# A windowed attention and two expert layers on one core: the opening's instructions in a listed order, and a planner with re-measured costs

## The chip, the cores and the metric

The kernel runs on one core of one Trainium2 chip. The metric is the device time of one launch in microseconds (us). Five engines work beside each other, each taking its own instructions strictly in the order in which the program lists them: TensorE (PE in the profile; PEld is its weight load), VectorE (DVE), ScalarE (ACT), GpSimd (POOL) and SyncE (SP, which here only issues DMAs). An instruction that waits for another engine holds up everything listed behind it on its own engine.

## The reference

```
# attention: q, k, v are (2, 8, 768, 64); block = 32, window = 16
k_sum = max of k over blocks of 32 keys;  v_sum = mean of v over the same blocks
scores_l = q k^T / 8, kept only where |i - j| < 16
scores_s = q k_sum^T / 8 + log(32)
a = softmax over both together;  x = a [v ; v_sum]          # 1536 tokens x 512
# first layer
h = x @ w_in (512 x 2048);  x = (h * tanh(softplus(h))) @ w_out (2048 x 512)
# second layer
out = ((x @ w_a) * (x @ w_b)) @ w_out2                       # inner width 1536
```

The weights arrive as 64-bit floats and are brought to 32 bits on the chip, since nothing is computed on the host.

## The kernel before, in words

The 1536 tokens are cut into six groups g0 to g5 of 256 tokens, three for each of the two batch entries; the eight heads form four pairs p0 to p3. One unit of attention is a group and a head pair. A unit goes through all engines in turn:

- its keys and queries come by DMA (`load_k`, `load_q`), and VectorE takes the maximum over key blocks (L462, `prep_k`, one for each head pair of a batch entry);
- TensorE makes the scores (`batch_s`, L567 for the window, L571 for the block maxima): one call for each pair in g0, one for two pairs in the later groups;
- VectorE adds the mask and takes the row minimum, four times (L588); ScalarE makes four exponentials with row sums (L594); VectorE adds an epsilon (L597), inverts (L599) and multiplies (L601);
- TensorE transposes the weights (L626), ScalarE or VectorE copies them out of PSUM (L377 and L378, the two alternatives of `copy`), and TensorE multiplies them with v (L638, in g0 also L651 for the block means, which come from L492 through `keep_v`);
- ScalarE and VectorE split the result into a high and a low part (L377, L668), because every later product is made as three products of rounded parts.

The first layer runs on the finished groups: L897 is x times a chunk of w_in, L927 the activation Mish on ScalarE, L930 its split on VectorE, L944 the product with w_out. Its first four chunks are multiplied directly and interleave with the attention of later groups; the other chunks and the whole second layer use a scheme with seven products for eight (L1076, L1121, L1229). Each weight chunk is loaded raw, converted to 32 bits (L688 or L691 on ScalarE, L693 and L696 on VectorE) and split (L377 on ScalarE, L708 on VectorE).

ScalarE evaluates Mish and the exponential from different tables, and changing between them is an instruction of its own (ACT_TABLE_LOAD). At the start the program asks for the exponential's table once (`preload_act_table_set`, L426), so that the load lies before the first scores.

No order is written by hand. Every operation is handed to a class `Plan` (`add`) with a due time (`key`), its cost, what it reads and writes and the engines that may do it. `emit` then plays the program through with those costs: each engine takes, among the operations that are ready at its moment, the one with the smallest key, and that sets the instruction order for good. Where TensorE would be idle before a fixed moment (`fill_end`, 12.48 us of the planner's time), `emit` puts in dummy products (L434, `fill`) that keep it active; eight of them (`warm_up`) open the program. These dummies stand in the program unconditionally: the chip executes them whether TensorE would have waited or not. The constants at the head of `Plan` are the planner's picture of the chip: hops between engines, DMA delay and rate, table load, the clock of TensorE (`WARM`, `ham_end`).

## Time and profile before

| | us |
|---|---|
| median of 3 runs | 595.59 (595.39 to 595.86) |
| profiled execution, first to last instruction (span) | 593.8 |
| rest of a launch around the span (595.6 less 593.8) | 1.8 |
| PE busy in the span | 586.6 |
| DVE busy | 489.2 |
| ACT busy | 318.8 |

The profile does not give a measured time of its own for the profiled execution beside its span; the 1.8 us are the difference to the median of the runs. "Busy" for PE counts the dummies and also matmuls that run at a lower clock or wait inside the array, so a busy PE is not a PE that gets on.

### The profile page before, as it was taken

To read this page: it belongs to the slowest core of one execution; us is meant where nothing else is said; L and a number is where in the kernel's file an instruction comes from. 1 tells how busy PE (TensorE), PEld (TensorE's weight loads), DVE (VectorE), ACT (ScalarE), POOL (GpSimd) and SP (SyncE) were. 2 spreads that over 40 slices of the span, in tenths; PEclk is the share of its full clock that TensorE was granted. 3 is DMA by queue.
4 is the path that set the end of the run, shared out by engine and by line. 5 is a ranking of instruction groups with operands and counts; after the bars stand their busy time and mean duration, and the time that the engine had idled before them with its cause. 6 is when DMAs were issued, how large, how long until landed. Compare 5 with 4: busy or idle time off the path is not lost.

```text
span 593.8 us, 10770 instructions
## 1 busy us (share of the span) xinstructions
PE 586.6 (99%) x4162; PEld 530.9 (89%) x4163; DVE 489.2 (82%) x1134; ACT 318.8 (54%) x711; POOL 6.7 (1%) x34
## 2 busy tenths in 40 slices
PE   9999999999999999999999999999999999999998
PEld 5788788889898899989999999999898999999896
DVE  6899999999999988979799998858686876855443
ACT  5699999457555555455376655444262434433030
POOL 3000000000000000000000000000000000000000
PEclk9899999999999999999999999999999999999999
DMA  9997700222233221222003133230122212300202
GB/s 282 348 345 221 224 20 3 71 72 72 71 107 106 73 71 72 72 71 72 0 1 100 43 107 111 103 107 20 52 72 71 108 35 72 107 0 2 89 18 107
DMA packets 22288, 54.89 MB, mean 92 GB/s; under 512 B 1917, under 2 KB 8061, under 8 KB 22237
## 3 DMA queue, kind: packets, MB, share of 16 engines
q1 hardware_dynamic: 22236, 54.21, 27.8%
q8 instruction: 32, 0.52, 0.4%
q14 instruction: 20, 0.16, 0.1%
HBM read 50.07 MB, written 3.15 MB: 90 GB/s over the span
## 4 chain that ended last, share of the span: by engine, by line
PE 92%; ACT 3%; DVE 3%; DMA 1%; issue 1%; ACTq 0%
PE bank L1076 44%; PE bank L1121 17%; PE bank L1229 17%; PE bank L944 5%; PE bank L897 4%; ACT attn L594 2%; PE bank L567 1%; PE bank L638 1%; DMA attn<-attn 1%; PE bank L626 1%; PE bank L434 1%; DVE attn L588 1%; ACT L927 1%; ACT rounded L377 0%; PE bank L571 0%
## 5 line engine op out<-in xcount | busy, mean ns | idle before, releaser
L1076 PE MATMUL bank<-rounded,wext 128*128 128x384 f32 x1176 | 213.8, 335 | 0.0
L1076 PEld LDWEIGHTS bank<-rounded,wext 128*128 128x128 f32 x1176 | 205.7, 188 | 3.5
L377 ACT CAST rounded<-arena 128x384 fp32r<-128x384 f32 (+2 forms) x145 | 80.8, 568 | 88.9 <-PE bank L1229 37.4
L1121 PE MATMUL bank<-rounded,wext 128*128 128x512 f32 (+1 forms) x456 | 104.7, 380 | 0.0
L1229 PE MATMUL bank<-wext,rounded 128*128 128x512 f32 (+2 forms) x441 | 100.0, 386 | 0.0
L1089 DVE TENSOR_TENSOR arena<-arena,bank 128x384 f32<-128x384 f32 x132 | 71.8, 550 | 31.2 <-PE bank L1076 23.1
L1229 PEld LDWEIGHTS bank<-wext,rounded 128*128 128x128 f32 x441 | 82.0, 188 | 16.3
L1121 PEld LDWEIGHTS bank<-rounded,wext 128*128 128x128 f32 x456 | 83.9, 188 | 12.6
L1085 ACT COPY arena<-bank 128x384 f32<-128x384 f32 x108 | 51.5, 478 | 56.5 <-PE bank L1076 53.8
L377 ACT CAST wext<-arena 128x512 fp32r<-128x512 f32 (+1 forms) x80 | 49.0, 621 | 33.2 <-PE bank L1076 12.7
L1076 PE MATMUL bank<-rounded 128*128 128x384 f32 x336 | 61.1, 335 | 0.0
L1076 PEld LDWEIGHTS bank<-rounded 128*128 128x128 f32 x336 | 58.5, 188 | 0.2
L1125 DVE TENSOR_TENSOR arena<-bank,arena 128x512 f32<-128x512 f32 (+1 forms) x76 | 49.9, 658 | 10.0 <-PE bank L1121 9.9
L1248 DVE TENSOR_TENSOR arena<-bank,arena 128x512 f32<-128x512 f32 (+2 forms) x37 | 25.0, 677 | 34.5 <-PE bank L1229 34.5
L708 DVE TENSOR_TENSOR wext<-arena,wext 128x512 fp32r<-128x512 f32 (+1 forms) x80 | 49.8, 639 | 0.7 <-ACT wext L377 0.3
L696 DVE SCALAR_TENSOR_TENSOR arena<-arena 128x512 uint32<-128x512 uint32 x68 | 46.6, 689 | 2.3 <-ACT arena L688 0.4
L708 DVE TENSOR_TENSOR rounded<-arena,rounded 128x384 fp32r<-128x384 f32 (+2 forms) x72 | 40.9, 583 | 4.8 <-ACT rounded L377 4.3
L594 ACT ACTIVATE attn<-attn 128x120 f32<-128x120 f32 x96 | 36.7, 386 | 7.6 <-DVE attn L588 7.5
L944 PE MATMUL bank<-rounded 128*128 128x512 f32 (+1 forms) x168 | 37.1, 367 | 0.0
L688 ACT ACTIVATE arena<-arena 128x512 f32<-128x512 f32 x38 | 25.8, 680 | 17.7 <-DMA arena<-in_w_out_dram 9.4
L897 PE MATMUL bank<-rounded 128*128 128x512 f32 (+1 forms) x168 | 35.3, 363 | 0.0
L897 PEld LDWEIGHTS bank<-rounded 128*128 128x128 f32 x168 | 28.1, 189 | 4.7
(75 smaller groups left out, 546.3 us busy)
## 6 DMA issues: line engine op xcount, KB each, us to landing
arena<-in_w_out_dram SPq DMA_DIRECT2D x28, 512.0 KB, 3.3
arena<-in_w_in_dram SPq DMA_DIRECT2D x16, 512.0 KB, 3.9
arena<-in_w_a_dram SPq DMA_DIRECT2D x12, 512.0 KB, 4.1
arena<-in_w_b_dram SPq DMA_DIRECT2D x12, 512.0 KB, 3.3
arena<-in_kT_dram SPq DMA_DIRECT2D x8, 384.0 KB, 9.6
out_dram<-arena SPq DMA_DIRECT2D x11, 256.0 KB, 2.0
attn<-in_qT_dram SPq DMA_DIRECT2D x5, 512.0 KB, 8.7
attn<-in_v_dram SPq DMA_DIRECT2D x3, 768.0 KB, 7.3
```

The costliest lines, as they stand in the source:

```text
L377: alts = [("ACT", act_us(n), lambda env: nc.scalar.copy(out=dst(env), in_=src(env))), ("DVE", dve2_us(n) if fast else dve_us(n), lambda en ...
L594: act(key, SW + 90, lambda env, x=x: nc.scalar.activation(out=s[:, x, :], in_=s[:, x, :], func=AF.Exp, scale=-1.0, bias=negm[:, x:x + 1], ...
L696: dve(key, 512, lambda env: nc.vector.scalar_tensor_tensor(out=f.bitcast(U32), in0=hw.bitcast(U32), scalar=3, in1=f.bitcast(U32), op0=ALU. ...
L708: dve(key, n, lambda env: nc.vector.tensor_sub(out=r32(lo[0]()), in0=src, in1=hi[0]()), r=rd + hi[1], w=lo[1])
L897: nc.tensor.matmul(like(dst, b), lt, rt, start=(j == 0), stop=(j == 3 * KC - 1))
L944: nc.tensor.matmul(yp, lt, r32(rt), start=(fst and j == 0), stop=(lst and j == 2))
L1076: nc.tensor.matmul(dst, lt, r32(rt), start=(start and i == 0 and j == 0), stop=(last and i == 1 and j == 2), skip_group_check=True)
L1085: act(k, TN, lambda env: nc.scalar.copy(out=dst[0], in_=bank[env[nm[z]]][:, 0:TN]), w=[nm[z]] + dst[1])
L1089: dve(k, TN, lambda env: op(out=dst[0], in0=dst[0], in1=bank[env[nm[z]]][:, 0:TN]), w=dst[1] + [nm[z]], free=[nm[z]] if free else [])
L1121: nc.tensor.matmul(dst, lt, rt, start=(q == 0), stop=(q == 5))
L1125: dve(k + 1.2, n, lambda env: nc.vector.tensor_add(acc, bank[env[yn]][:, 0:n].rearrange(*shape[2], **shape[3]), acc), w=[yn] + ak, free=[yn])
L1229: nc.tensor.matmul(dst, lt, rt, start=(opens and j == 0), stop=(closes and j == n_mm - 1))
```

## The change

Two things change. First, `Plan` gets a table `ORDER` with a list of operation numbers for each engine. While an engine's list lasts, `emit` no longer chooses among the ready operations: the engine takes the next number of its list and waits for it if it is not ready. Operations in no list are not offered to any engine that still has a list to work off. The lists hold 125 operations for PE, 315 for DVE, 186 for ACT, 7 for POOL and 55 for SP; they cover the attention and the beginning of the first layer. After them the old rule goes on. In the lists an operation that ScalarE or VectorE may do is fixed to one of the two. SyncE's backlog limit is off while its list lasts, and dummies are put in on PE only while the next listed operation is waiting.

Second, the planner's constants and some durations are set to other values. They change no instruction by themselves, only what the planner believes, and so the placing of the dummies and the order after the lists. The explicit preload of the exponential's table, for instance, is now believed to cost 0.02 us instead of 1.3.

```
-    HOP = {"PE": 0.25, "DVE": 0.14, "ACT": 0.14, "POOL": 0.1, "SP": 0.05}
+    HOP = {"PE": 0.05, "DVE": 0.13, "ACT": 0.13, "POOL": 0.1, "SP": 0.05}
+    BEGIN = {"DVE": 0.93, "PE": 0.5, "ACT": 0.8}
-    DMA_LEAD, DMA_TAIL, DMA_RAMP = 0.62, 2.18, 8.0
+    DMA_LEAD, DMA_TAIL, DMA_RAMP = 0.62, 1.87, 8.3
-    TABLE, TABLE_PENALTY = 1.3, 5.37
-    WARM, PAGE, PE_LEAD, FETCH, FETCH_BUSY = 0.34, 256, 64, (6.4, 2.6), 46.0
+    TABLE, TABLE_PENALTY = 1.283, 5.37
+    WARM, PAGE, PE_LEAD, FETCH, FETCH_BUSY = 0.45, 256, 64, (6.4, 2.6), 46.0
...
-        ham_cold, ham_busy, ham_over, ham_end = True, 0.0, 0.0, 3.4133
+        ham_cold, ham_busy, ham_over, ham_end = True, 0.0, 0.0, 2.034
+        given = {e: list(reversed(q)) for e, q in dict(self.order).items()}
+        listed = {i: e for e, q in given.items() for i in q}
...
+                if given.get(e):
+                    i = given[e][-1]
+                    wq, rq = ([], []) if missing[i] else ([], [(0.0, i)]) if ready_at[i] <= t else ([(ready_at[i], 0.0, i)], [])
...
-                    until = dma_free - self.BACKLOG
+                    until = 0.0 if given.get(e) else dma_free - self.BACKLOG
...
+ORDER = {
...
+    "ACT": [
+        44, 45, 43, 42, 54, 57, 56, 55, 3, 87, 68, 69, 66, 81, 67, 80, 79, 78, 466, 105, 469, 33,
...
-    pl = Plan()
+    pl = Plan(ORDER)
...
-    pl.add(-1.0, [("ACT", 1.3, lambda env: nc.scalar.preload_act_table_set("exp_and_others"))], table="exp")
+    pl.add(-1.0, [("ACT", 0.02, lambda env: nc.scalar.preload_act_table_set("exp_and_others"))], table="exp")
```

Lines of the changed kernel stand 57 further down from the table on (L594 is L651 there, L588 is L645).

**ScalarE at the start.** In the line of ACT above, operation 3 is the preload. The exponentials are L594 (before) and L651 (after), the copy out of PSUM L377 and L434. Before:

```order
L426 ACT_TABLE_LOAD
L594 ACTIVATE attn<-attn 128x120 x8
L377 COPY attn<-bank_68 120x512
L594 ACTIVATE attn<-attn 128x120 x8
L688 ACTIVATE arena<-arena 128x512
```

After:

```order
L651 ACT_TABLE_LOAD
L651 ACTIVATE attn<-attn 128x120 x8
L483 ACT_TABLE_LOAD
L434 COPY attn<-bank_68 120x512
L651 ACTIVATE attn<-attn 128x120 x8
L745 ACTIVATE arena<-arena 128x512
```

The preload has moved behind the first eight exponentials (p0 and p1 of g0). Since the exponentials now come first, the build places a load of the same table ahead of them by itself, so there are two loads where there was one; the second stands ahead of the copy of p0's transposed weights and of the exponentials of p2 and p3.

**VectorE at the start.** TENSOR_REDUCE is the maximum over key blocks, ISA is the mask and minimum (its 128x1 rows read the minimum out), TENSOR_SCALAR, RECIPROCAL and TENSOR_TENSOR are the epsilon, the inverse and the multiply; banks 1 and 2 hold p0's scores, 3 and 4 p1's, 5 p2's. Before:

```order
L462 TENSOR_REDUCE attn_71<-arena_70 128x24
L588 ISA attn_71<-bank1_62,attn_71 128x120
L588 ISA attn_71 128x1
L588 ISA attn_71<-bank2_63,attn_71 128x120
L588 ISA attn_71 128x1
L462 TENSOR_REDUCE attn_71<-arena_70 128x24
L588 ISA attn_71<-bank1_62,attn_71 128x120
L588 ISA attn_71 128x1
L588 ISA attn_71<-bank2_63,attn_71 128x120
L588 ISA attn_71 128x1
L588 ISA attn_71<-bank3_64,attn_71 128x120
```

After:

```order
L519 TENSOR_REDUCE attn_71<-arena_70 128x24 x2
L645 ISA attn_71<-bank1_62,attn_71 128x120
L645 ISA attn_71 128x1
L645 ISA attn_71<-bank1_62,attn_71 128x120
L645 ISA attn_71 128x1
L645 ISA attn_71<-bank2_63,attn_71 128x120
L645 ISA attn_71 128x1
L645 ISA attn_71<-bank2_63,attn_71 128x120
L645 ISA attn_71 128x1
L519 TENSOR_REDUCE attn_71<-arena_70 128x24
```

The maximum over p1's keys has moved ahead of all four mask operations of p0. SyncE's list meanwhile puts the keys of p2 ahead of the queries of p1; before, keys and queries alternated.

**TensorE at the end of g0 and the start of g1.** L638 and L651 (before), L695 and L708 (after) are the products with v and with the block means, L492 and L549 make the block means, L626 and L683 transpose; L567 and L624 are scores. Before:

```order
L626 MATMUL bank_67<-attn 120x128 x4
L638 MATMUL bank_61<-arena,attn 64x64 x8
L492 MATMUL bank_65<-arena,attn 24x128 x8
L638 MATMUL bank_62<-arena,attn 64x64 x8
L651 MATMUL bank_68<-attn 64x256 x2
L651 MATMUL bank_63<-attn 64x256 x2
L651 MATMUL bank_61<-arena,attn 64x256 x2
L651 MATMUL bank_62<-arena,attn 64x256 x2
L567 MATMUL bank_64<-arena,attn 64x96
```

After:

```order
L683 MATMUL bank_66<-attn 120x128 x4
L549 MATMUL bank_64<-arena,attn 24x128 x8
L695 MATMUL bank_62<-arena,attn 64x64 x8
L708 MATMUL bank_68<-attn 64x256 x2
L708 MATMUL bank_63<-attn 64x256 x2
L695 MATMUL bank_65<-arena,attn 64x64 x8
L708 MATMUL bank_65<-arena,attn 64x256 x2
L624 MATMUL bank_61<-arena,attn 64x96
```

The four products with the block means no longer stand in one run: one product with v stands among them, and the fourth comes between the two score calls of g1.

Further on, where the trace of before has the product with v that starts at 64.53 us, PE's list puts a score call (L567, L571) ahead of that product (L638) instead of behind it. Behind the lists, from the first L1076 on, PE's order stays as it was but for single blocks of six L1076 that stand one block earlier or later.

## Rows read from the trace of the kernel before

**Rows 1.** The profile's page: span, and busy time of each engine.

```profile
span 593.8 us, 10770 instructions
PE 586.6 (99%) x4162; PEld 530.9 (89%) x4163; DVE 489.2 (82%) x1134; ACT 318.8 (54%) x711; POOL 6.7 (1%) x34
```

**Rows 2.** Chain that ended last: start us, us, what.

```profile
129.62 16.72 PE bank L1076 x96
...
578.20 12.80 PE bank L1229 x63
```

**Rows 3.** Waits of PE: line, what it waited for, total us, times, longest.

```profile
PE bank L626 <- DVE attn L601: 1.6, 3, 0.6
...
PE bank L638 <- DMA attn<-attn: 0.5, 1, 0.5
...
PE bank L626 <- ACT arena L927: 0.4, 1, 0.4
```

**Rows 4.** Windows: length, busy (count) of PE, PEld, DVE, ACT, POOL; clock, DMA share, GB/s.

```profile
3.00:6.00 3.00, 3.00 (x38) 1.41 (x37) 0.95 (x1) 0.00 (x0) 2.40 (x12) 1.00 0.94 294
...
22.51:25.93 3.42, 3.42 (x97) 3.37 (x96) 3.35 (x21) 1.72 (x9) 0.00 (x0) 0.50 1.09 378
25.00:30.00 5.00, 4.58 (x61) 4.32 (x54) 4.89 (x31) 5.00 (x24) 0.00 (x0) 0.91 1.07 305
30.00:35.00 5.00, 3.85 (x109) 3.33 (x108) 4.59 (x18) 4.95 (x14) 0.00 (x0) 1.00 1.05 312
50.00:60.00 10.00, 9.61 (x257) 8.15 (x246) 9.91 (x42) 9.94 (x26) 0.00 (x0) 1.00 0.64 207
60.00:70.00 10.00, 9.42 (x155) 7.67 (x155) 9.86 (x35) 9.95 (x32) 0.00 (x0) 1.00 0.64 181
```

**Rows 5.** Timeline of PE: start us, us, instruction, shapes, count, idle before.

```profile
17.37 0.62 PE L626 MATMUL bank<-attn 128*120 128x128 f32 x4 [0.18 <-ACT rounded L377]
...
19.88 1.08 PE L651 MATMUL bank<-attn 24*64 24x256 f32 x8
...
21.75 0.40 PE L567 MATMUL bank<-arena,attn 64*64 64x96 f32 x8
...
25.84 3.17 PE L897 MATMUL bank<-rounded 128*128 128x256 f32 x24
...
30.42 0.40 PE L567 MATMUL bank<-arena,attn 64*64 64x96 f32 x8
...
31.67 1.15 PE L638 MATMUL bank<-attn 120*64 120x64 f32 x32
```

**Rows 6.** Timeline of DVE, first 18 us.

```profile
4.15 0.95 DVE L462 TENSOR_REDUCE attn<-arena 128x24 f32<-128x768 f32 x1 [2.94 <-DMA arena<-in_kT_dram]
6.04 0.28 DVE L588 CUSTOM_DVE_ANT_0 attn<-bank,attn 128x120 f32<-128x120 f32 x1 [0.93 <-POOL attn L415]
...
6.63 0.95 DVE L462 TENSOR_REDUCE attn<-arena 128x24 f32<-128x768 f32 x1
...
16.57 0.65 DVE L601 TENSOR_TENSOR attn<-attn 128x480 f32<-128x480 f32 x1
```

**Rows 7.** Timeline of ACT in the opening.

```profile
0.81 1.28 ACT L426 ACT_TABLE_LOAD   x1 [0.81 <-PEq L1329]
...
11.35 0.58 ACT L377 COPY attn<-bank 120x512 f32<-120x512 f32 x1
...
14.86 0.38 ACT L594 ACTIVATE attn<-attn 128x120 f32<-128x120 f32 x1
...
24.54 0.40 ACT L594 ACTIVATE attn<-attn 128x120 f32<-128x120 f32 x1 [1.70 <-DVE attn L588]
...
31.67 0.19 ACT L594 ACTIVATION_READ_ACCUMULATOR attn<-attn 128x1 f32 x1
31.88 1.28 ACT L927 ACT_TABLE_LOAD   x1
33.17 0.66 ACT L927 ACTIVATE arena<-bank 128x256 f32<-128x256 f32 x2
```

More of the change, by code (lines that the diff above doesn't have):

```diff
@@ L67, in cells, with add @@
         return out
-    def add(self, key, alts, r=(), w=(), alloc=(), free=(), delay=0.0, table=None, duty=1.0, words=0):
+    def add(self, key, alts, r=(), w=(), alloc=(), free=(), delay=0.0, table=None, duty=1.0, words=0, lag=0.0):
         i = len(self.ops)
@@ L86, in add @@
         deps.discard(i)
-        self.ops.append((key, alts, deps, alloc, free, delay, table, duty, words))
+        self.ops.append((key, alts, deps, alloc, free, delay, table, duty, words, lag))
     def emit(self):
@@ L108, in emit @@
         ready = {e: [] for e in engines}
-        free_at = {e: 0.0 for e in engines}
+        free_at = {e: self.BEGIN.get(e, 0.0) for e in engines}
         bank_free, where, held = {b: 0.0 for b in range(8)}, {}, set()
         dma_free, landed, table, shape = 0.0, [], None, None
-        ham_cold, ham_busy, ham_over, ham_end = True, 0.0, 0.0, 3.4133
+        ham_cold, ham_busy, ham_over, ham_end = True, 0.0, 0.0, 2.034
         fetched, page_at = self.PE_LEAD, 0.0
+        given = {e: list(reversed(q)) for e, q in dict(self.order).items()}
+        listed = {i: e for e, q in given.items() for i in q}
         def arrive(i):
             for a in ops[i][1]:
-                heapq.heappush(waiting[a[0]], (ready_at[i], key[i], i))
+                if i not in listed:
+                    heapq.heappush(waiting[a[0]], (ready_at[i], key[i], i))
         for i in range(n):
@@ L162, in emit @@
                         pick, later = None, [until]
-                if pick is None and e == "PE" and ham_end > 3.5 and t < self.fill_end:
+                if pick is None and e == "PE" and ham_end > 3.5 and t < self.fill_end and (wq or not given.get(e)):
                     fb = [b for b in bank_free if b not in held and bank_free[b] <= t]
@@ L184, in emit @@
             else:
-                _, alts, _, alloc, free, delay, needs, duty, words = ops[i]
+                _, alts, _, alloc, free, delay, needs, duty, words, _ = ops[i]
                 _, cost, fn = next(a for a in alts if a[0] == e)
                 state[i] = 1
+                if given.get(e) and given[e][-1] == i:
+                    given[e].pop()
             for name, b in zip(alloc, bank):
@@ L203, in emit @@
                     cost *= 2.0
-                    duty *= 0.5
                 ham_busy += duty * min(cost, ham_end - t)
@@ L218, in emit @@
             if delay:
-                dma_free = max(dma_free, end + self.DMA_LEAD) + delay * (1.35 if 2.0 < dma_free < self.DMA_RAMP else 1.0)
+                dma_free = max(dma_free, end + self.DMA_LEAD) + delay * (1.255 if 2.0 < dma_free < self.DMA_RAMP else 1.0)
                 end = dma_free + self.DMA_TAIL
@@ L228, in emit @@
                 same = len(ops[u][1]) == 1 and ops[u][1][0][0] == e
-                ready_at[u] = max(ready_at[u], end + (self.SAME if same else self.HOP[e]))
+                ready_at[u] = max(ready_at[u], end + (self.SAME if same else self.HOP[e] + ops[u][9]))
                 missing[u] -= 1
@@ L574, in batch_s @@
         rd = [x for p in ps for x in (sb(q_o[g % NQ] + p * GT, GT), sb(kt_o[p], SK), ("kpad", p), sb(ksum_o[p], NB))]
-        pe(key, 0.58 * len(ps), mm, words=64 * len(ps), duty=0.69, table="quarters", r=rd, w=names + sks, alloc=tuple(names))
+        pe(key, 0.58 * len(ps), mm, words=64 * len(ps), duty=0.69, lag=-0.28, table="quarters", r=rd, w=names + sks, alloc=tuple(names))
         for k, p in enumerate(ps):
```

19 lines of the change are left out of this document (11 added, 8 removed), and 40 rows, old and new, of the table ORDER.

## The prediction

> **What bounds the kernel now.** I read the page first, then the chain, the waits of PE, windows of the opening, and the timelines of single engines there. The page says that PE is busy for 586.6 of 593.8 us [rows 1], so the kernel is the length of PE's work plus what PE loses. The chain says where it loses nothing: from 129.62 us to the last products at 578.20 us it is PE all through, and 96 L1076 take 16.72 us, 174 ns each [rows 2]. A reordering of the opening can gain there only by letting this stretch begin earlier; it shifts as a block. What PE loses lies ahead of it. The waits name 2.5 us behind VectorE, ScalarE and one DMA [rows 3]; the windows put 0.42 of them at 25 to 30, 1.15 at 30 to 35, 0.39 at 50 to 60 and 0.58 us at 60 to 70 (length less PE's busy time) [rows 4], 2.54 us in all. One loss does not show as idle time: from 22.51 to 25.93 us the granted clock is 0.50, the lower of the two levels, 1.2 GHz [rows 4]. The two score calls of g1 and what follows take from 21.75 to 25.84, 4.09 us, while the same kind of call at 2.4 GHz takes 1.25 us (30.42 to 31.67) [rows 5]; two of them should take 2.50, so 1.59 us are lost. From 25 to 70 us VectorE and ScalarE are busy for nearly the whole of every window [rows 4], and that is why PE waits there. The most that the change can take away behind 20 us is therefore 2.54 + 1.59 = 4.1 us.
>
> **The change, part by part.** First g0, where one chain of latencies runs through four engines.
>
> VectorE now takes the key maximum of p1 before p0's four mask operations. Before, it stood between them, began at 6.63 and took 0.95 us; p0's first mask operation began at 6.04 [rows 6]. In the new order the mask operations wait for p1's keys. When these land the trace bounds from both sides: not before p0's keys (4.15) and not after 6.63 [rows 6]. Between lie p0's queries and p1's keys, 0.13 and 0.39 MB, which at the 294 GB/s of that window [rows 4] is 0.524 / 0.294 = 1.8 us, so about 5.9 us; I take that. The masks then begin at 5.9 + 0.95 = 6.9 us instead of 6.04 (bounds 6.1 and 7.6), but they run in one piece, so that p0's last one comes out near where it was. p1's queries have been put behind p2's keys, another 0.39 MB, some 1.2 us; p1's scores begin near 8.0 instead of before the maximum of p1 had ended, and p2's a little earlier than they did. Up to here nothing is gained or lost by more than half a microsecond, and the ten dummies behind p2's scores lie in time in which PE would wait for p0's multiply.
>
> ScalarE then meets the second table load. A load took 1.28 us each of the times that rows show it [rows 7]. A load of a table that is already there does not occur in the trace: it costs between 0 (if the engine skips it) and 1.28 us. I take 1.28, since the loads of both tables took the same. The Trainium skill, page "ScalarE: Activation LUTs", section "What ACT_TABLE_LOAD costs", says that a load copies the whole slot whatever the table is, and adds a drain of about 1.38 us to every switch, 2.66 us in all; by that the new load would cost 2.66 us and the time below would be 1.4 us longer. The trace does not agree with the drain: the last read before a load ends at 31.86, the load runs from 31.88 to 33.16, and the next operation starts at 33.17 [rows 7]. Nothing hides this load. Ahead of it stands p1's last exponential, behind it p0's copy and the eight exponentials of p2 and p3. The copy started at 11.35 and the last exponential at 14.86 before [rows 7]. Now p1's last mask operation comes behind p0's multiply, near 10.7 us, its exponential ends near 11.5, the load near 12.8 and the copy near 13.3; eight exponentials of 0.38 us [rows 7] end at 16.3 instead of 15.24, 1.1 us later. Two multiplies follow at once, because VectorE's list no longer puts a weight conversion between them: the last ends near 17.9 instead of at 16.57 + 0.65 = 17.22 [rows 6], 0.7 us later. The transpose behind it, at 17.37 before [rows 5], moves to about 18.1. From there to g1's scores the old order needed 21.75 - 17.37 = 4.4 us [rows 5]. In the new order the same pieces stand there but for one of the four products with the block means, which took 21.75 - 19.88 = 1.87 us together [rows 5], 0.47 each: 3.9 us. So g1's scores start near 22.0 us, against 21.75: I book +0.2 us for the opening up to here, with bounds of -1.1 (the load skipped) and +1.0 (keys at 6.63 and no gain from the tighter order).
>
> Second, the clock. What PE did before it fell was the run of eight-by-two products with the block means (24 x 64 tiles, 19.88 to 21.75 us [rows 5]). The new order breaks this run with a product with v and a score call, but the same small pieces fill the same few microseconds, and by the later copy PE has more idle time at 14 to 18 us than it had. The bounds are -1.6 us (the clock stays at 2.4 GHz) and +1.6 us (a second stretch of that length at 1.2 GHz). I take 0, because the instructions nearest to the fall are the same ones. The Trainium skill, "TensorE: Matmul & The Clock Gate", section "HAM oscillation — how this bites in real kernels", has the clock fall after idle gaps; here it fell with PE busy throughout, so by that rule alone before would have kept its clock.
>
> Third, the waits behind 25 us. Between the first mask operation of g1 and its fourth multiply, VectorE's two lists hold the same 35 operations but for one (a cast of 256 columns before, a subtraction of 256 columns now), so the transposes L626 there, which wait for the multiplies (1.6 us in rows 3), wait as before: g1 starts no earlier. Of the 1.57 us at 25 to 35 I take away only a third, 0.5 us, for PE's other fillers. At 64.53 us PE waited 0.53 us for a DMA with the product L638 at its head; in the new order a score call of 1.25 us stands ahead of it and covers that: -0.5. For the wait of 0.39 us before a transpose at 50 to 60 us, behind a Mish [rows 3, 4], three products L944 now stand ahead of the transposes instead of behind them; I take away half of it. Sum -1.2 us; bounds 0 (each wait is followed by another) and -2.54 (all gone).
>
> Between 70 us and the long stretch PE does not wait now. The new order puts VectorE's multiplies for g4 and g5 further back in its list, behind conversions and sums for the next layer, so part of what PE gains may be given back there; between 0 and the gain itself, and I take 0.3 us.
>
> Sum: +0.2 + 0 - 1.2 + 0.3 = -0.7 us. Against the profiled execution that is a span of 593.1 us; the 595.59 us of the runs are 1.8 us above the span, and the change touches nothing outside it, so the forecast is 594.9 us.
>
> **The rivals.** (a) *The listed order holds: the clock stays up and most waits go.* For it speaks that the breaks in the run of block-mean products lie exactly where the clock fell, and that a score call now stands where PE waited for the DMA. Against it, VectorE and ScalarE have no less work from 25 to 70 us, and both are full. Its time: -1.6 for the clock, -2.0 of the waits, +0.2: 592.2 us. With the second load skipped it would be 591.
>
> (b) *The second load decides, and the result is slower.* The place is ScalarE between p1's exponentials and p0's copy. PE, which has no dummies behind 12.48 us of the planner's time, idles at 13 to 18 us until the copies and multiplies of p1 to p3 come; if this also brings a stretch of half clock while g0's chain runs (+1.6), and the two full engines carry the delay of g0 (+1.0) on through g1 and g2 with no wait shortened, the sum is +2.0 to +2.6: 597.9 us. It decides from the point where g1's scores start later than about 23 us. For it: the load has no cover, and the planner counted it as 0.02 us. Against it: ScalarE stood idle for 1.70 us before g1's first exponential at 24.54 [rows 7], and a delay of g0 can be taken up there.
>
> (c) *It does nothing:* the two full engines set when PE may go on, whatever the order, and g0's loss and the saved waits cancel: 595.6 us.
>
> **How the numbers follow.** A measurement of this kernel can tell about 0.2%, 1.2 us, from no change. Chances: forecast 0.40, (a) 0.27, (b) 0.18, (c) 0.15. The forecast's own range is 593.6 to 596.2 us. Faster than 594.4: nearly all of (a) and a third of the forecast, 0.26 + 0.14 = 0.40. Slower than 596.8: most of (b), and a little of the others, 0.19. The rest, 0.41, is no change. The range that leaves out 2 in 10 runs from 592.0 to 597.6 us.
>
> **What would show it.** In the new profile: a second ACT_TABLE_LOAD of about 1.28 us on ScalarE between 11 and 13 us, and p0's copy behind it; p0's first mask operation near 6.9 us; the last multiply of g0 near 17.9 and g1's first score call near 22.0 us; the place of clock 0.50; PE's waits for L601; no wait of L638 for a DMA; and the start of the first L1076, 129.62 us now, which should move by as much as the whole time does. The forecast is wrong if the clock stays at full level and L1076 starts before 127.5 us, if the second load takes no time, or if L1076 starts after 131 us.

## The result, and the profile after

The changed kernel takes 599.89 us (median of 5 runs, 599.28 to 600.81) against 595.59: a ratio of 1.0071 with the interval 1.0059 to 1.0083. It is 0.7% slower, and the forecast of 594.9 with its range up to 597.6 is wrong. Lines of the changed kernel are those of before plus 57: L1076 is now L1133, L638 is L695, L588 is L645.

The page of the changed kernel, to be set beside [rows 1]:

```profile
span 599.1 us, 10732 instructions
...
PE 587.6 (98%) x4162; PEld 528.9 (88%) x4162; DVE 486.4 (81%) x1125; ACT 324.7 (54%) x721; POOL 6.7 (1%) x34
```

PE is busy 1.0 us longer and idle 4.3 us longer, nearly all of that ahead of the long stretch: a product that waits inside the stretch counts as busy. The profiled run is the slowest of the five (600.81 us), so its span shows 5.3 us of loss where the medians show 4.3. The chain of waits says where the loss lies. Its first and last long pieces, as in [rows 2]:

```profile
132.69 16.20 PE bank L1133 x90
...
583.39 12.80 PE bank L1286 x63
```

The long stretch begins 3.07 us later (132.69 against 129.62), and its last products end at 596.19 instead of 591.00, 5.19 later. So 3.07 us are lost ahead of the stretch and 2.12 inside it. The prediction held that the stretch shifts as a block. The waits of PE's weight loads behind 132 us (line, what it waited for, total us, times, longest) show that it does not; before has none from 128 us on:

```profile
PEld bank L1133 <- ACT arena L1142: 1.6, 5, 0.4
PEld bank L1133 <- DVE arena L1146: 0.9, 4, 0.3
```

L1142 and L1146 empty the banks that L1133 fills. Nine times a product's weight load stands at the head of PE's queue before the bank is empty.

Ahead of the stretch, the opening first. VectorE's timeline (start us, us, instruction, idle before it), to be set beside [rows 6]:

```profile
5.90 0.95 DVE L519 TENSOR_REDUCE attn<-arena 128x24 f32<-128x768 f32 x1 [1.05 <-DMA arena<-in_kT_dram]
6.77 0.27 DVE L645 CUSTOM_DVE_ANT_0 attn<-bank,attn 128x120 f32<-128x120 f32 x1
...
9.77 0.28 DVE L645 CUSTOM_DVE_ANT_0 attn<-bank,attn 128x120 f32<-128x120 f32 x1 [0.38 <-PE bank L628]
...
18.32 1.23 DVE L658 TENSOR_TENSOR attn<-attn 128x480 f32<-128x480 f32 x2
```

p1's keys landed at 5.90 and p0's masks began at 6.77, as forecast (5.9 and 6.9). p1's masks (9.77) and all behind them came late; the last multiply of g0 ends at 19.55. ScalarE, beside [rows 7]:

```profile
12.79 1.28 ACT L483 ACT_TABLE_LOAD   x1
14.09 0.58 ACT L434 COPY attn<-bank 120x512 f32<-120x512 f32 x1
...
17.39 0.38 ACT L651 ACTIVATE attn<-attn 128x120 f32<-128x120 f32 x1
...
26.13 0.40 ACT L651 ACTIVATE attn<-attn 128x120 f32<-128x120 f32 x1
```

The load of the table that is already there takes the full 1.28 us. PE, beside [rows 5]:

```profile
8.95 0.40 PE L624 MATMUL bank<-arena,attn 64*64 64x96 f32 x8 [1.87 <-DMA attn<-in_qT_dram]
...
19.12 1.13 PE L683 MATMUL bank<-attn 128*120 128x128 f32 x8 [0.89 <-DVE attn L658]
...
23.92 0.40 PE L624 MATMUL bank<-arena,attn 64*64 64x96 f32 x8
...
27.00 1.22 PE L954 MATMUL bank<-rounded 128*128 128x256 f32 x8
```

g1's scores start 2.17 us later than before. The first product of the first layer (27.00) is only 1.16 us late, because the two score calls no longer run at half clock. From there to the first L1133 PE takes 105.53 us where before took 103.62 (25.84 to 129.46): it is idle for 3.43 instead of 2.54 us, and the same products take 1.02 us more (102.10 instead of 101.08 us busy).

Then the transfers. Windows of the changed kernel, columns as in [rows 4]:

```profile
20.00:25.00 5.00, 4.72 (x123) 3.21 (x124) 4.37 (x9) 4.21 (x11) 0.52 (x1) 1.00 1.00 329
25.00:30.00 5.00, 5.00 (x108) 4.48 (x100) 5.00 (x33) 4.50 (x21) 0.00 (x0) 1.00 0.71 203
30.00:35.00 5.00, 4.04 (x109) 3.41 (x108) 4.93 (x22) 4.89 (x18) 0.00 (x0) 1.00 0.71 222
...
45.00:50.00 5.00, 5.00 (x35) 4.51 (x34) 3.50 (x16) 4.16 (x15) 0.00 (x0) 1.00 1.00 234
50.00:55.00 5.00, 3.71 (x126) 3.25 (x128) 4.97 (x15) 4.94 (x9) 0.00 (x0) 1.00 1.04 348
```

From 25 to 35 us the DMA engines were full before (1.07 and 1.05 [rows 4]) and moved 305 and 312 GB/s; now they stand at 0.71 with 203 and 222. At 45 to 50 us VectorE, the full engine of this part, is idle for 1.5 us, and at 50 to 55 PE for 1.3. SyncE's timeline and its waits name the gap:

```profile
27.39 0.40 SPq L421 DMA_DIRECT2D attn<-in_qT_dram  x1
33.00 0.34 SPq L421 DMA_DIRECT2D arena<-in_kT_dram  x1
...
34.66 1.11 SPq L421 DMA_DIRECT2D attn<-in_v_dram  x2
...
40.39 0.86 SPq L421 DMA_DIRECT2D arena<-in_kT_dram  x2
...
43.82 0.84 SPq L421 DMA_DIRECT2D attn<-attn  x1
```

```profile
SPq L421 <- PE bank L624: 5.1, 1, 5.1
```

From 27.8 us the listed next transfer is a block of the second batch's keys, whose buffer g2's first score call still reads until 33.0; SyncE waits 5.1 us with it, and g2's v windows (34.66), which need not wait, stand behind it. What answers to that on VectorE and PE, from VectorE's timeline and the waits of PE:

```profile
49.68 0.95 DVE L519 TENSOR_REDUCE attn<-arena 128x24 f32<-128x768 f32 x1 [1.50 <-DMA arena<-in_kT_dram]
```

```profile
PE bank L683 <- DVE attn L658: 2.5, 4, 0.9
PE bank L624 <- DMA attn<-in_qT_dram: 1.9, 1, 1.9
PE bank L695 <- DMA attn<-in_v_dram: 1.3, 1, 1.3
```

Against [rows 3], PE's waits for the multiply have grown from 1.6 to 2.5 us, the wait for a DMA from 0.5 to 1.3. It stands before g2's first product with v (from 50.68 to 51.97 us), and the profile puts it down to the last of several things that this product needs. Another is VectorE's copy of the transposed weights, which stands in VectorE's list behind the maximum over the late keys and ended at 51.44 us:

```profile
50.75 0.69 DVE L435 COPY attn<-bank 120x512 f32<-120x512 f32 x1
```

So the late keys alone would have kept PE waiting for more than half of that time.

### The profile page after: what moved, and what is told of

Read it like the earlier page. It is cut to its first block, busy times and chain, and to the rows that moved or that the text cites. A ratio compares the mean times of both kernels' runs of the same rounds, so it can differ in the third digit from the quotient of the medians.

```text
span 599.1 us, 10732 instructions
## 1 busy us (share of the span) xinstructions
PE 587.6 (98%) x4162; PEld 528.9 (88%) x4162; DVE 486.4 (81%) x1125; ACT 324.7 (54%) x721; POOL 6.7 (1%) x34
## 4 chain that ended last, share of the span: by engine, by line
PE 87%; DVE 8%; DMA 3%; ACT 1%; issue 1%; SPq 0%; DVEq 0%
PE bank L1133 43%; PE bank L1286 16%; PE bank L1178 16%; PE bank L1001 5%; PE bank L954 4%; DMA arena<-in_kT_dram 1%; DVE attn L645 1%; DVE attn L658 1%; DMA attn<-in_qT_dram 1%; PE bank L695 1%; PE bank L683 1%; DVE attn L435 1%; PE bank L624 1%; ACT rounded L434 1%; DVE arena L753 1%; DVE rounded L765 1%
## 5 line engine op out<-in xcount | busy, mean ns | idle before, releaser
L1133 PE MATMUL bank<-rounded,wext 128*128 128x384 f32 x1176 | 214.0, 336 | 0.1
L1133 PEld LDWEIGHTS bank<-rounded,wext 128*128 128x128 f32 x1176 | 205.7, 188 | 4.7 <-ACT arena L1142 1.2
L434 ACT CAST rounded<-arena 128x384 fp32r<-128x384 f32 (+3 forms) x146 | 80.5, 565 | 91.8 <-PE bank L1286 42.1
L1146 DVE TENSOR_TENSOR arena<-arena,bank 128x384 f32<-128x384 f32 x132 | 71.7, 548 | 33.9 <-PE bank L1133 26.2
L1142 ACT COPY arena<-bank 128x384 f32<-128x384 f32 x108 | 51.4, 478 | 53.3 <-PE bank L1133 50.6
L434 ACT CAST wext<-arena 128x512 fp32r<-128x512 f32 (+1 forms) x80 | 49.2, 621 | 31.4 <-PE bank L1133 17.9
L1133 PE MATMUL bank<-rounded 128*128 128x384 f32 x336 | 61.0, 337 | 0.0
L1133 PEld LDWEIGHTS bank<-rounded 128*128 128x128 f32 x336 | 58.2, 188 | 1.5 <-DVE arena L1146 0.8
L1182 DVE TENSOR_TENSOR arena<-bank,arena 128x512 f32<-128x512 f32 (+1 forms) x76 | 49.8, 656 | 11.5 <-PE bank L1178 11.4
L651 ACT ACTIVATE attn<-attn 128x120 f32<-128x120 f32 x96 | 37.0, 388 | 9.3 <-DVE attn L645 9.0
L1001 PE MATMUL bank<-rounded 128*128 128x512 f32 (+1 forms) x168 | 37.9, 370 | 0.0
L954 PE MATMUL bank<-rounded 128*128 128x512 f32 (+1 forms) x168 | 34.6, 362 | 0.0
L954 PEld LDWEIGHTS bank<-rounded 128*128 128x128 f32 x168 | 28.1, 189 | 4.6
```

The costliest lines, as they stand in the source:

```text
L434: alts = [("ACT", act_us(n), lambda env: nc.scalar.copy(out=dst(env), in_=src(env))), ("DVE", dve2_us(n) if fast else dve_us(n), lambda en ...
L651: act(key, SW + 103, lambda env, x=x: nc.scalar.activation(out=s[:, x, :], in_=s[:, x, :], func=AF.Exp, scale=-1.0, bias=negm[:, x:x + 1], ...
L954: nc.tensor.matmul(like(dst, b), lt, rt, start=(j == 0), stop=(j == 3 * KC - 1))
L1001: nc.tensor.matmul(yp, lt, r32(rt), start=(fst and j == 0), stop=(lst and j == 2))
L1133: nc.tensor.matmul(dst, lt, r32(rt), start=(start and i == 0 and j == 0), stop=(last and i == 1 and j == 2), skip_group_check=True)
L1142: act(k, TN, lambda env: nc.scalar.copy(out=dst[0], in_=bank[env[nm[z]]][:, 0:TN]), w=[nm[z]] + dst[1])
```

## The experiments

All kernels of this table ran beside the kernel before, whose median was 595.6 to 596.0 us. "Scores" is the start of g1's first score call, "first L1133" and "stretch" the start of that product and the time from there to the start of the last one, all by PE's timeline of the one profiled run (the chain's times lie 0.16 us later).

| kernel | median us | ratio and interval | scores | first L1133 | stretch |
|---|---|---|---|---|---|
| before | 595.59 | 1 | 21.75 | 129.46 | 461.25 |
| changed | 599.89 | 1.0071 (1.0059 to 1.0083) | 23.92 | 132.53 | 463.37 |
| e12 changed, again | 600.76 | 1.0086 (1.0071 to 1.0101) | 23.64 | 133.09 | 463.41 |
| e2 costs only | 602.41 | 1.0109 (1.0094 to 1.0124) | 22.39 | 134.87 | 462.97 |
| e3 lists only | 599.90 | 1.0070 (1.0055 to 1.0085) | 23.89 | 134.03 | 461.52 |
| e5 HOP as before | 599.28 | 1.0059 (1.0035 to 1.0083) | 23.86 | 131.53* | 465.02* |
| e17 lists and HOP only | 600.20 | 1.0080 (1.0063 to 1.0096) | 23.89 | 131.42 | 463.29 |
| e1 preload first | 599.25 | 1.0057 (1.0039 to 1.0074) | 22.39 | 129.71 | 463.38 |
| e7 second load in before | 596.33 | 1.0010 (1.0000 to 1.0020) | 22.27 | 129.76 | 461.27 |
| e4 p1's queries first | 600.50 | 1.0071 (1.0054 to 1.0088) | 23.24 | 133.91 | 463.34 |
| e6 preload first, HOP | 599.57 | 1.0075 (1.0049 to 1.0100) | 23.32 | 129.28* | 464.97* |
| e8 SyncE's list cut | 609.78 | 1.0234 (1.0219 to 1.0250) | 22.97 | 141.54 | 463.40 |
| e9 g3's windows ahead | 606.43 | 1.0172 (1.0152 to 1.0193) | 22.93 | 135.62 | 463.36 |
| e10 that, preload first | 605.67 | 1.0162 (1.0145 to 1.0179) | 23.05 | 138.54 | 463.38 |
| e11 that, old costs | 606.79 | 1.0173 (1.0142 to 1.0205) | 22.82 | 139.22 | 461.50 |
| e13 g2's transfers ahead | 599.75 | 1.0067 (1.0044 to 1.0089) | 23.90 | 131.41 | 463.38 |
| e14 opening as before | 601.62 | 1.0086 (1.0056 to 1.0116) | 22.52 | 129.92 | 463.40 |
| e15 both | 600.69 | 1.0081 (1.0058 to 1.0105) | 22.05 | 130.64 | 463.35 |
| e16 both, old costs | 599.13 | 1.0055 (1.0038 to 1.0072) | 22.24 | 133.38 | 461.54 |

In e3, e11, e16 and e17 the lines are one further (L1134), in e8 two less (L1131). (*) Twelve L1001 of 229 ns stand behind the first L1133 instead of ahead of it: 2.74 us belong on the other side.

### The lists or the costs

e2 leaves the lists out:

```diff
-    pl = Plan(ORDER)
+    pl = Plan()
```

> The changed kernel's new planner costs with empty lists: the planner chooses everywhere, as before the change, but with the new durations. Theory B (the new costs, above all the short hop behind TensorE, place L1133 blocks so close behind the copies that free their PSUM bank that weight loads wait): the stretch from the first L1133 to the last product gets about 2 us longer than before's 461.5, as in the changed kernel, and the time is 1.5 to 3 us above before (597 to 598.5) even without the lists. Rival C (the lists make the late stretch longer, by the state in which they leave the buffers): the late stretch stays at 461.5 us and the time within 1 us of 595.6.

e3 keeps the lists and puts every cost, lag and starting value back to those of before:

```diff
-    BEGIN = {"DVE": 0.93, "PE": 0.5, "ACT": 0.8}
+    BEGIN = {}
...
-        ham_cold, ham_busy, ham_over, ham_end = True, 0.0, 0.0, 2.034
+        ham_cold, ham_busy, ham_over, ham_end = True, 0.0, 0.0, 3.4133
```

> The changed kernel with its lists but all planner costs, the clock's start and the lags set back to those of before. Theory B: the late stretch is 461.5 us again, and the time falls by about 2 us to 597.9; the first L1133 starts where it does in the changed kernel (132.5 us, give or take 0.5 for other dummies). Rival C: the late stretch stays near 463.7 us and the time near 599.9.

Both stretches came as theory B had them, and neither time did. The costs alone make the kernel slower still (602.41 instead of 597 to 598.5, with the clock at 0.50 from 23.6 to 30.4 us in the profiled run), so the lists win back part of what the costs lose. On the old costs the stretch is 461.50 to 461.54 us under the lists, on the new ones 462.97 to 463.41 in every kernel but the two marked, whatever stands ahead of it. PE's weight loads in e3 wait once behind 128 us:

```profile
PEld bank L1134 <- ACT arena L1143: 0.3, 1, 0.3
```

Of the 2.12 us lost inside the stretch 1.85 thus come from the costs (463.37 against 461.52). The loss ahead of it is there with the lists alone, but also with the costs alone: e2 starts the stretch 5.4 us later than before. e3 lost more there than the changed kernel: its clock stood at 0.50 from 24.8 to 31.6 us, and all four of its runs have a mean clock of 0.993 or 0.994. So in the median the old costs gain nothing under the lists (599.90 against 599.89).

### Which cost

e5 is the changed kernel with one line of e3; e17 is e3 with that line the other way round:

```diff
-    HOP = {"PE": 0.05, "DVE": 0.13, "ACT": 0.13, "POOL": 0.1, "SP": 0.05}
+    HOP = {"PE": 0.25, "DVE": 0.14, "ACT": 0.14, "POOL": 0.1, "SP": 0.05}
```

> The changed kernel with one line of costs as before: HOP, what the planner counts from an engine's end to a waiting engine's start, 0.25 us again for PE's results instead of 0.05 (and 0.14 instead of 0.13 for VectorE and ScalarE). The lists, and so the opening, are those of the changed kernel. Theory B1 (the 2.1 us that the long stretch lost come from HOP: with 0.05 us the planner puts a weight load of L1133 too close behind the copy that empties its bank): the stretch from the first L1133 to the last product 461.2 to 461.8 us (463.4 with the changed costs, 461.3 before), no PEld wait of L1133 behind L1142 or L1146, time 597.5 to 598.3. Theory B2 (another cost does it, such as the lag of the transposes or the removed halving of duty): the stretch stays at 463 us or more and the time near 599.9. In both the first L1133 starts at 131 to 133 us.

> The lists on the costs of the kernel before, with the new HOP as the only changed cost (0.05 us instead of 0.25 from the end of a product of PE to an engine that waits for it). The loss in the long stretch is taken as its length less the length of its matmuls (174 ns for 384 columns, 229 ns for 512). Theory (HOP makes about half of the loss by itself: the planner lets an engine take a product 0.2 us before PE has ended it, and gives the bank to PE too early): the loss is 1.6 to 2.2 us, against 0.77 in e3. Rival (HOP matters only with the other new costs): it stays within 0.3 of 0.77. The time is 598.5 to 602 either way, since the opening decides it.

e17, waits of PE's weight loads behind 128 us:

```profile
PEld bank L1134 <- ACT arena L1143: 2.0, 5, 0.5
PEld bank L1134 <- DVE arena L1147: 0.3, 2, 0.2
```

With HOP as its only new cost the stretch is 1.77 us longer than in e3 (463.29 against 461.52), nearly as much as in the changed kernel (1.85): more than the half that the theory gave HOP, so HOP can make this loss by itself. e5 missed its 461.2 to 461.8: less the twelve L1001 its stretch is 462.28, and 0.76 us more than in e3 remain, with other waits. So the other new costs move the planner's order there as well, but are not needed for the loss. HOP is what the planner counts from the end of a product to the start of an engine that waits for it. That with 0.05 us it hands a bank out 0.2 us too early is the likely way; the runs show the line and the waits, not the planner's reason.

### The second load and the opening

e1 lists the preload first:

```diff
-        44, 45, 43, 42, 54, 57, 56, 55, 3, 87, 68, 69, 66, 81, 67, 80, 79, 78, 466, 105, 469, 33,
+        3, 44, 45, 43, 42, 54, 57, 56, 55, 87, 68, 69, 66, 81, 67, 80, 79, 78, 466, 105, 469, 33,
```

> The changed kernel with one edit: the preload of the exponential's table (operation 3) at the head of ScalarE's list, so that one load is left, at 0.8 us; dummies move a little. Theory A (the second load lies on g0's path without cover and its 1.28 us reach the end): ScalarE's copy of p0 starts at about 12.9 instead of 14.09 us, g1's first scores near 22.7 instead of 23.92, and the time falls by 1.0 to 1.3 us, from 599.9 to about 598.7. Rival (late keys and queries set the pace of g0, the load only fills a wait): copy earlier, but g1's scores move by less than 0.4 us and the time stays within 0.4 us of 599.9.

e7 is the kernel before, in its old order, with the load behind p1's last exponential:

```diff
-            act(key, SW + 90, lambda env, x=x: nc.scalar.activation(
+            act(key, SW + 90, lambda env, x=x: (nc.scalar.activation(
                 out=s[:, x, :], in_=s[:, x, :], func=AF.Exp, scale=-1.0, bias=negm[:, x:x + 1],
-                accum_out=l[:, x:x + 1]), ptr=1, r=[("negm", i, x)], w=[("l", i, x), ("e", i, x)], table="exp")
+                accum_out=l[:, x:x + 1]), (g, p, x) == (0, 1, GU - 1) and nc.scalar.preload_act_table_set("exp_and_others")), ptr=1, r=[("negm", i, x)], w=[("l", i, x), ("e", i, x)], table="exp")
```

> The kernel before with one instruction added and every other in its old place: a second load of the exp table on ScalarE, right behind the eighth exponential of g0 and ahead of p0's copy, where the changed kernel has it. This measures the second load by itself, in the old order. Theory A (the load alone delays g1 and all behind it): p0's copy near 12.6 instead of 11.35, g1's scores 1.0 to 1.3 us later than 21.75, first L1076 0.8 to 1.5 us later, time 596.6 to 597.3. Rival (ScalarE's and VectorE's free time between 17 and 25 us takes it up, and the lists lose by their order): first L1076 within 0.4 us of 129.5 and the time within 0.4 us of the kernel before.

e7's ScalarE and PE:

```profile
10.94 1.28 ACT L596 ACT_TABLE_LOAD   x1
12.23 0.58 ACT L377 COPY attn<-bank 120x512 f32<-120x512 f32 x1
```

```profile
22.27 0.40 PE L567 MATMUL bank<-arena,attn 64*64 64x96 f32 x8
```

The copy moves from 11.35 to 12.23, g1's scores by 0.52, the first L1076 by 0.30, the time by 0.1%: of 1.28 us a quarter to a third arrives, at the edge of what can be told from nothing. (e7's profiled run has no stretch of half clock, unlike that of before, so the 0.30 us are not the load's alone.) e1's profiled run, its shortest, has one load, brings g1's scores 1.5 us earlier and starts the stretch at 129.71, nearly as early as before; but its median gains 0.64 us. The load is real, and in the medians small: it does not explain 4 us.

e4 lists p1's queries (15) ahead of p2's keys (10); e14 does that, lists the preload first and puts p1's key maximum (9) behind p0's masks (38 to 41):

```diff
-        6, 14, 8, 10, 15, 16, 12, 17, 20, 21, 22, 25, 26, 465, 27, 28, 445, 18, 455, 24, 23, 85,
+        6, 14, 8, 15, 10, 16, 12, 17, 20, 21, 22, 25, 26, 465, 27, 28, 445, 18, 455, 24, 23, 85,
...
-        4, 7, 9, 38, 39, 40, 41, 11, 52, 50, 53, 62, 46, 47, 48, 51, 13, 58, 64, 59, 60, 65, 76, 63,
+        4, 7, 38, 39, 40, 41, 9, 11, 52, 50, 53, 62, 46, 47, 48, 51, 13, 58, 64, 59, 60, 65, 76, 63,
```

> The changed kernel with two entries of SyncE's list exchanged: p1's queries ahead of p2's keys, keys and queries alternate as before. Theory D (p1's scores at 8.95 instead of 7.41 us come from this place in the queue and are handed on): p1's scores start near 7.5 us, ScalarE's exponentials of p1 about 1 us earlier, and the time falls by 0.5 to 1.2 us. Rival (VectorE's order decides, its maximum over p2's keys and p0's masks stand ahead of p1's masks): p1's scores start earlier but p0's multiply does not, and the time stays within 0.4 us of 599.9.

> The changed kernel with the opening's three moved pieces back in their old order: the table load first in ScalarE's list, p1's queries ahead of p2's keys in SyncE's, p1's key maximum behind p0's masks in VectorE's. Theory (the opening's own order loses 1.5 to 2 us up to g1's scores): g1's scores at 21.8 to 22.6 us instead of 23.6 to 23.9, as before. If this carries through to the end: first L1133 1.2 to 2 us earlier and 598.0 to 599.0 us. If PE still waits at 48 to 52 us for the transfer of the block means, that wait grows by what g1 came earlier, and the time is 599.3 or more.

e4 gained 0.4 to 0.7 us at g1's scores and nothing in the end; its profiled run has the clock at 0.50 from 23.1 to 29.9. e14's profiled run is its shortest, 598.18 us: the clock is 1.00 and the stretch starts at 129.92; of its 2.7 us above before's span the stretch makes 2.1. In its three other runs the mean clock is 0.994 to 0.997, and they take 601.15 to 602.32. Against the profiled run of the changed kernel, its slowest, that run gains 2.6 us, against the others of the changed kernel with a mean clock of 0.999 or 1.0 (599.28 to 599.89) 1.1 to 1.7; the median shows nothing of it.

### The transfers

e8 cuts SyncE's list, and the planner chooses from there:

```diff
-        6, 14, 8, 10, 15, 16, 12, 17, 20, 21, 22, 25, 26, 465, 27, 28, 445, 18, 455, 24, 23, 85,
...
+        6, 14, 8, 10, 15, 16, 12, 17, 20, 21, 22, 25, 26, 465, 27, 28],
```

e9 moves g3's v windows and the second batch's v rows (176, 177, 179) ahead of a weight that waits for its buffer:

```diff
-        475, 36, 178, 160, 236, 509, 519, 112, 111, 529, 240, 234, 176, 113, 238, 177, 179, 539,
+        475, 36, 178, 160, 236, 509, 519, 112, 111, 176, 177, 179, 529, 240, 234, 113, 238, 539,
```

> The changed kernel with SyncE's list cut behind its first sixteen transfers (the opening's); from there on the planner chooses the transfers by due time again, while the lists of the other engines stay. Theory C (the listed order of transfers makes the v windows of g1 to g3 land late, since one transfer at the head of the list waits for its buffer, and that costs PE 1.3 us before a product with v near 50 us): no wait of L695 for in_v at 48 to 52 us, the first L1133 1.0 to 1.5 us earlier (131.0 to 131.5 against 132.5), time 598.4 to 599.2. Rival (what is late there is covered by the full engines anyway): the wait goes or moves and the first L1133 stays within 0.5 us, time 599.4 to 600.4.

> The changed kernel with three transfers of v windows moved ahead in SyncE's list: they no longer stand behind a weight transfer that waits 4 us for its buffer (issue at 35.7 to 37 us instead of 41.3, 45.3 and 46.1). Theory C (the listed order of transfers, and not the opening, makes half of the loss ahead of the long stretch): PE's wait of 1.3 us for in_v near 50.6 us is gone and the next 2 us with it lose less, first L1133 at 130.8 to 131.5 us against 132.5, time 0.8 to 1.5 us under the changed kernel of the same call. Rival (VectorE and ScalarE are full from 25 to 70 us and set the pace; what PE doesn't wait for here it waits for a few us later): the wait goes, another of about its length comes before 70 us, and the time is within 0.5 us of the changed kernel.

> The changed kernel itself, run again beside the other three, so that they are compared on one chip, and for a second profile of it: 599.3 to 600.8 us. It also tells how much of the place of the first L1133 (132.5 us in the first profile, of the longest of five runs) belongs to the single run: 131.0 to 132.5 is expected, with the long stretch at 463.4 us again.

Both made it far worse. In e8 a wait for a transfer from attn to attn has its own name, though before a later product, at 73.97 us (L693 there is L695):

```profile
PE bank L693 <- DMA attn<-attn: 5.2, 1, 5.2
```

and in e9 g2's first product with v comes at:

```profile
53.96 1.98 PE L695 MATMUL bank<-attn 120*64 120x64 f32 x32 [4.25 <-DVE attn L654]
```

The transfer from attn to attn spreads the block means over g2's v window. It is small (192 KB), but the changed kernel issues it at 43.82 behind a weight chunk, two blocks of keys and a v window, and PE goes on 8 us later. That PE's wait at 50.68 is for it is inferred: g2's own v window of 768 KB, issued at 34.66, had landed at 43.75. In e9 the product came 2 us later still, but there the profile names VectorE, which had waited for the keys that now stand behind three more transfers:

```profile
52.10 0.95 DVE L519 TENSOR_REDUCE attn<-arena 128x24 f32<-128x768 f32 x1 [4.89 <-DMA arena<-in_kT_dram]
```

So the keys count at least as much as the small transfer, and the theory of late v windows fell. e12 starts the stretch at 133.09, later than its 131.0 to 132.5. Its VectorE waits for the next keys still longer than in the first profile, and its PE's wait at g2's product (1.8 us) is put down to VectorE:

```profile
DVE attn L519 <- DMA arena<-in_kT_dram: 2.3, 1, 2.3
```

e13 moves g2's windows (112, 111) ahead of the keys that block SyncE (236), and the spread (113) ahead of a weight and two keys; e15 adds e14's edits:

```diff
-        475, 36, 178, 160, 236, 509, 519, 112, 111, 529, 240, 234, 176, 113, 238, 177, 179, 539,
+        475, 36, 178, 160, 112, 111, 236, 509, 519, 113, 529, 240, 234, 176, 238, 177, 179, 539,
```

> The changed kernel with SyncE's list altered at g2: the two transfers of g2's v windows ahead of the next batch's keys (which wait for their buffer until 33 us and hold up all behind them), and the transfer that spreads the block means right behind the two weights that follow, ahead of a weight and three keys. Theory D (PE's wait at 50.7 us is for this small transfer, which stands in the queue behind 1.5 to 2 MB): it is issued near 37 to 40 instead of 43.8 us and lands by 47; PE's wait before g2's first product with v is gone, this product starts at 49.5 to 50.8 instead of 51.97, and the first L1133 0.8 to 1.5 us earlier than in the changed kernel (131.3 to 132.3 by 132.5 and 133.1 of its two profiles); time 598.6 to 599.8. Rival (it is another transfer or the full engines): the product stays at 51.5 or later, or starts earlier and the first L1133 stays.

> Both edits. If the opening's delay and the late transfer are one loss behind the other (the transfer holds back whatever came earlier), only both together help: g1's scores at 22 us, g2's first product with v at 49 to 50.5, first L1133 at 129.5 to 130.8, time 597.0 to 598.2, of which 2.1 us above the kernel before are the long stretch. If neither is what loses, 599 or more.

e13's windows, SyncE and PE:

```profile
30.00:35.00 5.00, 4.04 (x109) 3.42 (x108) 4.93 (x22) 4.89 (x18) 0.00 (x0) 1.00 0.97 342
...
45.00:50.00 5.00, 5.00 (x34) 4.51 (x33) 4.86 (x19) 4.96 (x16) 0.00 (x0) 1.00 0.96 320
```

```profile
28.37 1.16 SPq L421 DMA_DIRECT2D attn<-in_v_dram  x2
32.99 0.35 SPq L421 DMA_DIRECT2D arena<-in_kT_dram  x1
...
36.34 0.83 SPq L421 DMA_DIRECT2D attn<-attn  x1
```

```profile
51.10 1.15 PE L695 MATMUL bank<-attn 120*64 120x64 f32 x32
```

The queue is filled while SyncE waits (0.97 instead of 0.71 at 30 to 35 us), VectorE's wait for the keys and PE's for the means are gone, and the stretch starts 1.1 us earlier than in the first profile of the changed kernel, 1.7 earlier than in the second, with g0 and g1's scores where they were. Between the first L954 and the first L1133 PE is busy for the same time, and idle for 2.33 instead of 3.43 us (the changed kernel, then e13):

```profile
27.00:132.53 105.53, 102.10 (x1319) 86.15 (x1314) 101.42 (x351) 89.88 (x253) 1.03 (x2) 1.00 0.47 142
```

```profile
26.98:131.41 104.43, 102.10 (x1320) 86.25 (x1313) 101.58 (x351) 89.65 (x254) 1.03 (x2) 1.00 0.45 143
```

So in these profiles the queue behind the blocked entry costs PE 1.1 us. e13 does not tell the keys from the spread, and it is one profile: e17, with SyncE's list as in the changed kernel but no wait of VectorE for these keys, starts its stretch at 131.42 too. In the medians the gain is within the intervals (599.75 against 599.89 and 600.76), and e15 does not add the two gains (130.64).

e6, e10, e11 and e16 put edits together, in search of one that is level with before:

> The changed kernel with two edits: the preload of the exp table stands first in ScalarE's list (one table load in the opening instead of two), and HOP is as before. If the two losses are separate and add (the second load 1 to 3 us at the first L1133; HOP 1.9 us in the long stretch), the first L1133 starts at 129.5 to 131 us, the stretch takes 461.2 to 461.8, and the time is 595.5 to 597.3: level with before. If the lists lose by themselves, apart from the load: first L1133 at 131.5 or later and 598 or more.

> Both edits at once: one table load in the opening (preload first) and the three v windows ahead. If the two are separate and add: first L1133 at 129 to 130.5 us, time 597.0 to 598.3. If the full engines set the pace, or g0's order is what loses: the same time as with the preload first alone, 599 or more.

> The lists with those two edits, on all the costs of the kernel before. If the long stretch's loss is due to the costs and the loss ahead of it to the two places mended, nothing is left of either: first L1133 at 129.5 to 131 us, stretch 461.2 to 461.8 us, time 595.3 to 596.8, level with before. If the lists bring a 6.8 us stretch of half clock at g1, as they did with the old costs, whatever ScalarE does: first L1133 at 132 or later and 597.8 to 599.5 us.

> Both edits on the costs of the kernel before: the long stretch at 461.5 us. If the long stretch, the opening and the transfer are the whole loss: 595.0 to 596.5 us. If a 6.8 us stretch of half clock comes at g1, as in the two earlier kernels with lists and old costs: 597 to 599 us, with the first L1133 at 131 to 133 us.

e10 and e11 carry e9's fault, with the clock at 0.50 for 10.2 us from 54.7; e11 has it there for 6.8 us from 24.0 as well, as its rival said. e6 and e16 missed too. e16 has the short stretch and g1's scores at 22.24, and loses 3.4 us between: VectorE waits 1.3 us for a w_in chunk, PE 1.4 us for a copy of ScalarE at the score call of 90.7 us. The lists may have been made for other durations from there on; no run shows that. No version was level with the kernel before.

## Why the prediction was wrong

**"It shifts as a block."** The step failed. It took the new costs for part of the opening, but they order the whole program. The stretch lost 2.12 us, 40% of the loss in the profiled run, outside every term of the sum; 1.85 of them are the costs' (against e3), and HOP by itself makes 1.77 (e17 against e3). The mark that the text set itself, a first L1076 after 131 us, was met (132.69 by the chain).

**g0, +0.2 booked; measured +2.17 at g1's scores.** The mechanism was right (masks 6.77 by 6.9, load 1.28 by 1.28), the size was off. p1's queries landed for scores at 8.95, not 8.0, so p1's last exponential and the load came 1.3 us later than forecast (12.79 by near 11.5). The copy ended at 14.67 by 13.3, the last multiply at 19.55 by 17.9. From there to g1's scores (23.92) the new order took 4.4 us where 4.1 were counted. So about half of the miss (0.95 of 1.92 us against the 22.0 forecast) was there when p1's queries came, and the upper bound of +1.0 was too low.

**The second load.** The 1.28 us were right. The Trainium skill, "ScalarE: Activation LUTs", "What ACT_TABLE_LOAD costs", has a load copy the whole slot whatever is in it: the trace agrees (12.79 to 14.07). Of the drain, which the Trainium skill gives there for a switch to a different set, it shows nothing, since the copy starts at 14.09. That nothing hides the load was wrong in the old order: e7 shows most of it covered. In the new order it held for g1's scores, which e1 brings 1.5 us earlier, but not for the median (0.64 us).

**The clock, 0 booked.** It stayed at 1.00 in the profile, as rival (a) had it, which counted 1.59 us for that. At the score calls they came, but not in the end: the kernel before, where it ran beside the experiments, takes 595.67 us in the median of its eleven runs with a mean clock of 0.999 or 1.0, and 595.88 in that of its 31 runs at 0.996 or 0.997. That VectorE has work enough there for PE's loss not to matter is the likely reason; no run shows it.

**The waits behind 25 us, -1.2 booked, and +0.3 up to the stretch.** Not gained: from the first L954 to the first L1133 the kernel lost 1.91 us (105.53 against 103.62). L638's wait for its DMA at 64.5 us went, as forecast, and one of 1.3 us came at 50.68. What the prediction did not weigh at all behind the opening is SyncE's list: which transfer stands at its head while its buffer is in use, and what queues behind it.

**Rival (b)** had the sign and its condition (scores after 23 us), 597.9 us. The delay of g0 that it named was there; its cause, the load, is worth 0.64 us in the median of e1.

What stays open is what the opening's order is worth in the median. e1 and e14 start the stretch 2.6 to 2.8 us earlier in their profiled runs, and their medians don't follow; with the lists the clock falls in some runs and not in others, and what decides this is not shown. The clock is not all of it either: e1's four runs, all at 1.0, take 597.98 to 600.49. And no edit brought back more than a small part of the 4.3 us in the median, so the parts above are shown in profiles of single runs, and what the whole loss in the median is made of stays open.

## What to carry over

A planner's cost is a part of the program wherever the planner still decides: changing it for the opening reorders the end as well, so time lists and costs apart. In a listed queue look for the entry that waits for a buffer, and ask what stands behind it that need not wait; here a busy queue that fell from 1.05 to 0.71 was the sign, and the bill came 15 us later on another engine. The wait alone is not the sign: in before SyncE waits 4.3 us for L638, and the queue stays at 1.04 (35 to 40 us). A mended profile of one run is no median: compare what the other runs did.

## What the runs showed of the hardware

A stretch of half clock costs much in one kernel and next to nothing in another. In before 3.4 us at 0.50 cost 0.2 us in the medians above; its one run at 0.994 took 598.07. In e5, whose profiled run has 6.8 us at 0.50 from 24.7, runs at a mean clock of 0.999 to 1.0 take 597.66, 598.40, 599.25 and 599.32 us, those at 0.994 and 0.991 take 601.46 and 601.78. But in e6 runs at 0.994 take 599.53 and 599.61 by 599.34 at 1.0, and in e16 those at 0.991 to 0.996 take 598.16 to 599.96 by 599.97. The same program falls or does not from run to run.

A small transfer pays for those ahead of it: 192 KB issued at 43.82 in the changed kernel were still out when PE waited at 50.68, 7 us later (inferred, as said above); issued at 36.34 in e13, they were no longer waited for.

A second load of the table that is already there took 1.28 us, as long as a load of another one.
